# Two token blocks on half the partitions each, for the last six chunk pairs of an SSD scan fused with a PReLU MLP

## The chip, the cores and the metric

The kernel runs on one core of a Trainium2 chip. The metric is the device time of one execution in microseconds; before the change it is 359.88 us, the median of three runs (359.64 to 360.04). The engines are called TensorE (PE in the profile; PEld is its weight loading), VectorE (DVE), ScalarE (ACT), GpSimd (POOL) and SyncE (SP, which issues nearly all DMAs).

## The reference

Two blocks follow each other. The first is a state-space scan over 4 batches, 8 heads, 768 tokens, with a head width D of 32 and a state width N of 16. The reference walks it in chunks of 32 tokens; any chunk length gives the same numbers:

```
la  = log(clip(a, 1e-6, 1));  cum = cumsum(la)           # within the chunk
L   = exp(cum[i] - cum[j]) where i >= j, else 0          # decays, lower triangle
M   = (C B^T) * L                                        # gram times decays
y   = M x + (C state) * exp(cum)                         # within, and carried in
state = exp(sum la) * state + sum_j B_j x_j exp(cum_end - cum_j)
```

The second takes y as a matrix of 3072 tokens by 256 features: `h = y @ w_in` (256 by 2048), `g = max(h, 0) + alpha * min(h, 0)`, `out = g @ w_out` (2048 by 256). All data is float32, and the kernel's matmuls are float32 too: TensorE runs each as two passes, each with a weight load and a matmul instruction of its own.

## The kernel before, in words

**Chunks and pairs.** The scan's chunk here has Q = 128 tokens. There are 24 chunks, and the kernel works on them two at a time: 12 pairs (`gp`, NP = 12), three to a batch, pair 0 to 2 of batch 0 and so on. For each chunk and head it needs a 128 by 128 triangle: the decays L (function `half_decays`, which calls `scan_half`, L470) come from a scan on VectorE along the row `a` spread over all partitions (tile `abc`), to which an identity is added so that the product starts at 1 on the diagonal; the gram C B^T (`products_bc`, L599) comes from TensorE, the eight heads lying on the partitions, 16 state rows each, two heads to a 32-row tile of the array; VectorE multiplies the two into `dec` (L609). One instruction of each step covers full squares, the half above the diagonal included, which is zero.

**Outputs and states.** `y` (L628 and L636) is the sum of the carried-in part (masked state times decayed C, 64-row by 32-column tiles) and `x` times `dec` (128-row by 32-column tiles), for two chunks and eight heads, in two PSUM banks; ScalarE copies it into `xT` (L645). `added` (L513) forms the state that a chunk adds, from `x` and the weighted B (`bn`, made by GpSimd in `pair_loads`, L418); `states` (L526, L523) updates the running state, and GpSimd masks it by heads (`sm`, L529). `c_decayed` (L563) and `spread_c` (L560) make two forms of C. `turn_bc` (L477) transposes B and C of the next pair on VectorE and begins its scans. The result of `added` for the next pair lies in the free half of the second of the two `y` banks (`beside`).

**The MLP** is the main load of TensorE. For the first 512 tokens it is plain (`hidden`, L853, and `output`, L891); for the other five groups of 512 tokens (`g` = 1 to 5) it uses seven block products in place of eight in both matrix products (`quad`, L977 for the first and `product`, L952, for the second). A group has four quads (`z` = 0 to 3) of about 13.6 us each; GpSimd makes the sums that the seven products need (`token_sums`, L932; L1024 and L1034 for g).

**Order.** It is written out by hand: each engine runs its instructions in the order in which the program emits them. `pair` is a generator; the table `steps` and the calls at `j == 5` in `after(j)` say between which products of a quad the stages of a pair are put. In a group the even pair's stages fall in quads 0 and 1 and the odd pair's in 1 to 3. The order on TensorE at a pair's end is: carried-in part, products with x, and right behind them the added state of the next pair.

**Loads.** `load_pair` puts a pair's DMAs on SP at the start of quads 0 and 2: the decays of C (`ap`), B and x of each chunk with tokens on partitions, B and C again as rows of tokens for the transpose (L184), and by `load_spread` the row `a` broadcast to all partitions (`abc`, L137). SP is in order too: from quad 1 of group 2 on, the output stores of `finish` (L1114) stand ahead of a load and wait for their data. `bns[ahead]` makes the weighted B in the same quad as the load, at j = 9; `turn_bc` follows in the next quad.

**Row preparation** for batches 2 and 3 (`rows_clamp(1)`, `rows_scan(1)`, `rows_out(1)`, later `rows_turn(1)`) writes the clamped rows to DRAM for the spread loads, and turns the products of decays to the end of each chunk onto partitions (`prt`), on TensorE with one copy by ScalarE.

The functions that the change touches follow as they are before it.

Of the kernel before, what the change touches and what calls it, by code (L numbers as in the profile page):

```python
# [22 lines left out]
def kernel(  # L23
# [51 lines left out]
    HT = GT // 2  # L75
    NB = 2
    WQ = 256
    assert H * N == P and HD == d_model and KC == 2 and R == CPB == 6
    assert NCH % GC == 0 and GT == 512 and NF % 8 == 0 and d_model <= WQ

# [47 lines left out]
    def load_a(t, b, c, eng=nc.sync):  # L128
        first = a[b, 0:1, c * Q : (c + 2) * Q]
        eng.dma_start(out=t, in_=bass.AP(tensor=first.tensor, offset=first.offset,  # L130
                                             ap=[[S, H], [0, N], [1, 2 * Q]]))

    def load_spread(gp, b, c):

        for k, t in enumerate(loads["p", gp][1]):
            rows = scratch["z", b // 2].rearrange("(b h c) t -> b c h t", b=2, h=H)[b % 2, c + k]
            nc.sync.dma_start(out=t.rearrange("p (h t) -> p h t", h=H),  # L137
                              in_=rows.unsqueeze(0).to_broadcast([P, H, Q]))

    def load_pair(gp, decays=True):  # L140


        b, c = divmod(2 * gp, CPB)
        turned = gp > GC
        nat = ldx.tile([P, 3, 2, H * N], F32, name="nat")
        xt = ldx.tile([P, 2, HD], F32, name="xt")

        ap = ldx.tile([P, 2 * Q], F32, name="ap")
        if gp == 0:
            load_a(ap, b, c)  # L150
        elif gp >= NB:
            rows = scratch["pf", b // 2].rearrange("(b h c) t -> b h (c t)", b=2, h=H)
            rows = rows[b % 2, :, c * Q : (c + 2) * Q]
            nc.sync.dma_start(out=ap, in_=rows.unsqueeze(1).to_broadcast([H, N, 2 * Q]))
        if gp == 0:
            load_rows(0, nc.scalar)
            nc.sync.dma_start(out=al_n, in_=moe_alpha.rearrange("(k p) -> k p", p=P))
        abc = []
        later = []
        for k in range(2):  # L160
            ts = slice((c + k) * Q, (c + k + 1) * Q)
            for i, src in enumerate((B,) if turned else (B, C)):
                nc.sync.dma_start(out=nat[:, i, k].rearrange("p (h n) -> p h n", h=H),  # L163
                                  in_=src[b, :, ts, :].rearrange("h p n -> p h n"))

            def load_x(k=k, ts=ts):
                nc.sync.dma_start(out=xt[:, k].rearrange("p (h d) -> p h d", h=H),
                                  in_=x[b, :, ts, :].rearrange("h p d -> p h d"))

            if gp < NB:  # L170
                later.append(load_x)
            else:
                load_x()
        for load_x in later:
            load_x()
        if gp == 0:
            loads["a", 1] = prep.tile([P, 2 * Q], F32, name="a1")
            load_a(loads["a", 1], b, c + 2)
        for i, src in enumerate((B, C) if turned else ()):


            for e in range(2):
                first = src[b, e : e + 1, c * Q : (c + 2) * Q, :]
                nc.sync.dma_start(out=nat[:, 1 + e, i],  # L184
                                  in_=bass.AP(tensor=first.tensor, offset=first.offset,
                                              ap=[[2 * S * N, P // 32], [8 * N, 32], [1, 8 * N]]))
        for k in range(2 if gp >= NB else 0):
            abc.append(lda.tile([P, H * Q], F32, name="abc"))
        loads["p", gp] = nat, abc, xt, ap
        if decays:  # L190
            load_spread(gp, b, c)
# [170 lines left out]
    def identity_bank():  # L362
# [3 lines left out]
        nc.scalar.copy(out=m5_bank[0][:, HT:], in_=ident_h[:, :HT])  # L366
        ident_p.append(m5_bank[0][:, HT:])

    def rows_clamp(i):
        rows = loads.pop(("r", i))  # L370
        d0 = prep.tile([RW, Q + 1], F32, name="r0")
        nc.vector.tensor_scalar(out=d0[:, :Q], in0=rows, scalar1=1e-6, scalar2=1.0,
                                op0=ALU.max, op1=ALU.min)
        held[i] = d0

    def rows_scan(i):

        d0 = held[i]
        nc.vector.memset(d0[:, Q:], 0.0)
        pr = prep.tile([RW, Q], F32, name="pr")  # L380
        nc.vector.tensor_tensor_scan(out=pr[:, ::-1], data0=d0[:, 1:][:, ::-1],
                                     data1=ends[:RW, ::-1], initial=0.0,
                                     op0=ALU.mult, op1=ALU.add)
        return pr
# [1 line left out]
    def rows_out(i):  # L386


        d0 = held.pop(i)[:, :Q]
        rpf = prep.tile([RW, Q], F32, name="rpf")  # L390
        nc.vector.tensor_tensor_scan(out=rpf, data0=d0, data1=zeros[:RW], initial=1.0,
                                     op0=ALU.mult, op1=ALU.add)
        nc.vector.memset(d0[:, :1], 0.0)
        for key, t in (("z", d0), ("pf", rpf)):
            scratch[key, i] = dr.tile([RW, Q], F32, name=f"{key}{i}")
            nc.sync.dma_start(out=scratch[key, i], in_=t)

    def rows_turn(i, pr):
# [2 lines left out]
        nc.tensor.transpose(ps[:, :RW], pr, ident[:RW, :RW])  # L401
        if i == 0:
            nc.tensor.transpose(ps[:, RW : RW + NF], al_n, ident[:NF, :NF])
        t = bat.tile([P, RW], F32, name="prt")
        nc.scalar.copy(out=t, in_=ps[:, :RW])
        if i == 0:
            nc.scalar.copy(out=alpha, in_=ps[:, RW : RW + NF])
        prt[i] = t
# [1 line left out]
    def pair_loads(gp):  # L410
# [3 lines left out]

        bn = work.tile([P, 2, H * N], F32, name="bn")
        i, bi = divmod(b, 2)
        pj = prt[i].rearrange("p (b h c) -> p b c h", b=2, h=H)[:, bi, c : c + 2]
        nc.gpsimd.tensor_tensor(  # L418
            out=bn.rearrange("p k (h n) -> p k h n", h=H),
            in0=nat[:, 0].rearrange("p k (h n) -> p k h n", h=H),  # L420
# [41 lines left out]

    bcs = {}
    decs = {}

    def scan_half(dec, abc, k, w):
        dv = dec.rearrange("p k h t -> p k (h t)")
        for i in range(2):
            hs = slice((2 * w + i) * 2 * Q, (2 * w + i + 1) * 2 * Q)
            nc.vector.tensor_tensor_scan(out=dv[:, k, hs], data0=abc[k][:, hs],  # L470
# [13 lines left out]
    def pair(gp):  # L484
# [2 lines left out]
        nat, abc, xt, ap = loads["p", gp]  # L487
        last = c + 2 == CPB
        fine = gp >= 2 * GC // 2
        dec = decs.pop(gp) if gp in decs else work.tile([P, 2, H, Q], F32, name="dec")  # L490
        dv = dec.rearrange("p k h t -> p k (h t)")
        begun_scans = gp in bcs

        def decays(k):
# [10 lines left out]
        new = work.tile([P, 2, 2 * D], F32, name="state")  # L505
        sm = work.tile([P, 2, P], F32, name="sm")

        def added(dps):
            dps = dps[:, : 4 * D].rearrange("p (k m) -> p k m", k=2)
            for k in range(nk):  # L510
                for r in range(4):
# [2 lines left out]
                                     xt[:, k, 2 * r * D : 2 * (r + 1) * D],  # L514
                                     start=True, stop=True, tile_position=(0, 32 * r),
                                     skip_group_check=True)
            return dps

        def states(dps):
            for k in range(nk):  # L520
                old = state.get(b)
                if old is None:
                    nc.scalar.copy(out=new[:, k], in_=dps[:, k])  # L523
                else:
                    e = (k + 1) * Q - 1
                    nc.vector.scalar_tensor_tensor(out=new[:, k], in0=old, scalar=pf[:, e : e + 1],  # L526
                                                   in1=dps[:, k], op0=ALU.mult, op1=ALU.add)
                state[b] = new[:, k]
            nc.gpsimd.tensor_tensor(  # L529
                out=sm[:, :nk].rearrange("p k (g m) -> p k g m", g=2),  # L530
                in0=new[:, :nk].unsqueeze(2).to_broadcast([P, nk, 2, 2 * D]),
                in1=hmask.rearrange("p (g m) -> p g m", g=2).unsqueeze(1)
                .to_broadcast([P, nk, 2, 2 * D]), op=ALU.mult)
            st.extend(sm[:, k] for k in range(nk))
            masked[b] = st[-1]

        if fine:
            bn = bns.pop(gp) if gp in bns else pair_loads(gp)
            dps = added(beside.pop(gp) if gp in beside else ss_tile()[:, : 2 * Q])
            yield  # L540
            states(dps)
            yield
# [17 lines left out]
                nc.scalar.mul(cz[:, e].rearrange("p k t -> p (k t)"), ct, par[:, e : e + 1])  # L560

        def c_decayed():
            nc.gpsimd.tensor_tensor(out=cd.rearrange("p k t -> p (k t)"), in0=ct, in1=pf,  # L563
                                    op=ALU.mult)

        if not fine:
            bn = bns.pop(gp) if gp in bns else pair_loads(gp)
# [23 lines left out]

        def products_bc():
            small = 2 if fine else 3
            gram = {r: (ss_tile() if r < small else spare())
                    .rearrange("p (k h t) -> p k h t", k=2, h=2) for r in range(4)}
            for k in range(2):
                for r in range(4):
                    rs = slice(32 * r, 32 * r + 32)
# [6 lines left out]
            yield  # L605
        gram = products_bc()
        for i, r in enumerate((2, 3, 0, 1) if fine else (3, 2, 1, 0)):
            hs = slice(2 * r, 2 * r + 2)
            nc.vector.tensor_tensor(out=dec[:, :, hs], in0=gram[r], in1=dec[:, :, hs], op=ALU.mult)  # L609
            if i == 1:  # L610
                yield
        if fine and gp + 1 < NP:
            turn_bc(gp + 1)
        yield

# [1 line left out]
        ys = [ss_tile() for w in range(KC)]  # L617
        y = [t[:, : 2 * Q].rearrange("p (k t) -> p k t", k=2) for t in ys]
        if fine:
            beside[gp + 1] = ys[1][:, 2 * Q :]  # L620
        begun = False
        for k in range(2):
            if st[k] is not None:
                for q in range(4):
# [4 lines left out]
                                         stop=False, tile_position=(64 * w, 32 * q),  # L629
                                         skip_group_check=True)  # L630
                begun = True
        for k in range(2):
            for w in range(KC):
                for q in range(4):
                    h = 4 * w + q
# [6 lines left out]
        if q == 0:  # L642
            xts[g] = xtp.tile([P, KC, GT], F32, name="xT")
        for w in range(KC):
            nc.scalar.copy(out=xts[g][:, w, q * Q : (q + 2) * Q],  # L645
                           in_=y[w].rearrange("p k t -> p (k t)"))


    def first_two():
# [573 lines left out]
    for i in range(NZ * (NG - 1)):  # L1223
# [3 lines left out]
        def after(j, g=g, z=z, i=i, nxt=nxt):  # L1227
# [5 lines left out]
                    output(NF - LATE + f, half)  # L1233
            if (i, j) in ((0, 13), (1, 2)):
                store_first(i)
            for args in late_sums.get((i, j), ()):
                weight_sums(*args)
            if g > 1 and z == 0 and j in (7, 11, 13, 14):
# [57 lines left out]
```

## Time and profile before

| what | value |
|---|---|
| median of 3 runs | 359.88 us (359.64 to 360.04) |
| the profiled execution | 360.17 us |
| its span, first to last instruction | 358.0 us |
| granted TensorE clock | 1.000 |
| TensorE busy | 351.5 us, 98% of the span |
| VectorE busy | 248.1 us, 69% |
| ScalarE busy | 169.6 us, 47% |
| GpSimd busy | 203.5 us, 57% |
| DMA, mean rate | 88 GB/s |
| the stretch of pairs 6 to 11 (146.2 to 291.2 us) | DVE busy 101.48, POOL 73.33, ACT 64.29 us of 145.00 |

Each line of the profile below names an engine, a source line, an operation with output<-input by the program's tile names, the shape of the array tile for TensorE (rows*columns), and partitions x elements. In a timeline line the first number is the start in us from the start of the span, the second the time to the end of the group, and x is the number of instructions in it. A matmul's end is modelled; the distance from one start to the next says how fast TensorE goes. Waits between engines go over semaphores; an instruction that has to wait for more than one is preceded by a wait instruction of its own, which the engine's sequencer carries out while the array still works on what was handed over before.

### The profile page before, as it was taken

What the parts mean: (1) busy time and instruction counts of PE and PEld (TensorE: products, weight loads), DVE (VectorE), ACT (ScalarE), POOL (GpSimd) and SP (SyncE); (2) the same over time, 40 slices, a digit from 0 to 9 for tenths busy, and PEclk for the clock granted to TensorE, in tenths of its full rate; (3) what the DMA queues carried; (4) which work ended last, traced back from release to release, by engine and by line L of the source; (5) the groups of instructions that cost most, each with busy time, mean ns of one, the idle gap of its engine ahead of it and who ended that gap; (6) DMA issues with size and microseconds to landing.
All of it is one profiled execution on the core that took longest, in us unless ns stands there. A gap on an engine that the chain in (4) does not pass through costs nothing.

```text
span 358.0 us, 6719 instructions
## 1 busy us (share of the span) xinstructions
PE 351.5 (98%) x2509; PEld 286.5 (80%) x2509; DVE 248.1 (69%) x465; ACT 169.6 (47%) x367; POOL 203.5 (57%) x212
## 2 busy tenths in 40 slices
PE   8899999999999999999999999999999999999996
PEld 7676665678788788888888888888888888888884
DVE  7987986998747857858748858667867633643363
ACT  3677576536256255355245454345445345443431
POOL 4976668589839755725655725646626535434521
PEclk9999999999999999999999999999999999999999
DMA  6999998408266202005505504603601001001004
GB/s 107 203 191 322 286 243 222 130 16 180 85 145 127 80 2 61 0 2 86 150 1 79 156 4 68 169 1 63 173 4 29 2 2 29 0 2 30 0 0 88
DMA packets 111015, 31.66 MB, mean 88 GB/s; under 512 B 79288, under 2 KB 106888, under 8 KB 110984
## 3 DMA queue, kind: packets, MB, share of 16 engines
q1 hardware_dynamic: 110056, 31.00, 37.1%
q8 instruction: 19, 0.31, 0.4%
q10 hardware_dynamic: 928, 0.25, 0.3%
q14 instruction: 12, 0.10, 0.1%
HBM read 27.89 MB, written 3.34 MB: 87 GB/s over the span
## 4 chain that ended last, share of the span: by engine, by line
PE 95%; POOL 1%; DMA 1%; SPq 1%; DVE 0%; issue 0%; ACT 0%; POOLq 0%
PE bank L952 34%; PE hp L977 28%; PE bank L891 8%; PE hp L853 6%; PE ss L977 6%; PE ss L636 3%; PE ss L599 2%; PE hp L868 2%; PE ss L628 1%; DMA nat<-in_C_dram 1%; PE bank L453 1%; PE ss L513 1%; PE hp L599 0%; SPq L163 0%; POOL w_in L291 0%
## 5 line engine op out<-in xcount | busy, mean ns | idle before, releaser
L1034 POOL TENSOR_TENSOR gt<-gt 128x512 f32<-128x512 f32 x58 | 74.2, 1280 | 21.2 <-DVE gt L962 16.4
L952 PE MATMUL bank<-gt,w_out 128*128 128x256 f32 x320 | 83.5, 381 | 0.0
L952 PEld LDWEIGHTS bank<-gt,w_out 128*128 128x128 f32 x320 | 60.1, 190 | 10.3 <-issue 2.3
L1024 POOL TENSOR_TENSOR gt<-gt 128x512 f32<-128x512 f32 x20 | 25.4, 1272 | 67.3 <-DVE gt L962 61.9
L962 DVE SCALAR_TENSOR_TENSOR gt<-hp,s_mul,gt 128x256 f32<-128x256 f32 x96 | 42.0, 479 | 29.9 <-ACT gt L960 27.3
L952 PE MATMUL bank<-gt,ws 128*128 128x256 f32 x240 | 59.5, 379 | 0.0
L960 ACT ACTIVATE gt<-hp,s_alpha 128x256 f32<-128x256 f32 x96 | 40.4, 472 | 39.3 <-PE hp L977 25.9
L952 PEld LDWEIGHTS bank<-gt,ws 128*128 128x128 f32 x240 | 45.6, 190 | 6.2
L470 DVE TENSOR_TENSOR_SCAN dec<-abc,bank 128x256 f32<-128x256 f32 x80 | 48.4, 659 | 0.0
L977 PE MATMUL hp<-xs,w_in 128*128 128x256 f32 x160 | 41.9, 384 | 0.0
L977 PE MATMUL hp<-xs,ws 128*128 128x256 f32 x160 | 41.2, 380 | 0.0
L1003 DVE TENSOR_TENSOR hp<-hp,u 128x512 f32<-128x512 f32 x20 | 13.9, 696 | 28.7 <-ACT u L1001 28.7
L977 PEld LDWEIGHTS hp<-xs,ws 128*128 128x128 f32 x160 | 30.3, 190 | 4.3 <-POOL xs L932 0.2
L977 PEld LDWEIGHTS hp<-xs,w_in 128*128 128x128 f32 x160 | 29.7, 190 | 4.6 <-issue 0.2
L891 PE MATMUL bank<-w_out,gt 128*128 128x256 f32 x128 | 31.1, 385 | 0.0
L891 PEld LDWEIGHTS bank<-w_out,gt 128*128 128x128 f32 x128 | 23.6, 190 | 6.8 <-issue 2.9
L977 PE MATMUL ss<-xT,w_in 128*128 128x256 f32 x96 | 24.6, 379 | 0.0
L853 PE MATMUL hp<-xT,w_in 128*128 128x512 f32 x48 | 22.7, 596 | 0.1
L529 POOL TENSOR_TENSOR sm<-state,bmask 128x256 f32<-128x256 f32 (+1 forms) x10 | 6.2, 620 | 29.0 <-DVE state L526 29.0
L992 ACT COPY m<-hp 128x512 f32<-128x512 f32 x8 | 4.7, 586 | 37.8 <-PE hp L977 37.8
L1001 ACT COPY u<-hp 128x512 f32<-128x512 f32 x20 | 11.7, 586 | 19.9 <-PE hp L977 19.9
L977 PE MATMUL hp<-xT,ws 128*128 128x256 f32 x80 | 20.5, 379 | 0.0
(179 smaller groups left out, 583.3 us busy)
## 6 DMA issues: line engine op xcount, KB each, us to landing
abc<-z SPq DMA_DIRECT2D x20, 512.0 KB
raw<-in_moe_w_in_dram SPq DMA_DIRECT2D x8, 512.0 KB
raw<-in_moe_w_out_dram SPq DMA_DIRECT2D x8, 512.0 KB
xt<-in_x_dram SPq DMA_DIRECT2D x24, 128.0 KB
nat<-in_B_dram SPq DMA_DIRECT2D x38, 64.0 KB
out_dram<-o_sb SPq DMA_DIRECT2D x32, 64.0 KB
nat<-in_C_dram SPq DMA_DIRECT2D x24, 64.0 KB
ap<-pf SPq DMA_DIRECT2D x11, 128.0 KB
```

The source lines that it names most:

```text
L470: nc.vector.tensor_tensor_scan(out=dv[:, k, hs], data0=abc[k][:, hs], data1=ident_p[0], initial=0.0, op0=ALU.mult, op1=ALU.add)
L636: nc.tensor.matmul(y[w][32 * q : 32 * q + 32, k], xt[:, k, h * D : (h + 1) * D], dec[:, k, h], start=False, stop=True, tile_position=(0, 3 ...
L853: nc.tensor.matmul(hp, w_in[:, k, f * P : (f + 1) * P], xts[g][:, k], start=(k == 0), stop=(k == KC - 1))
L891: nc.tensor.matmul(pos[0][t // 2][:, t % 2], gt[:, t * Q : (t + 1) * Q], w_out[:, f], start=(f == 0 and t % 2 == 0), stop=(f == NF - 1), s ...
L952: nc.tensor.matmul(ms[g][i][:, h], w, blocks[g, z][n][:, p], start=(q == 0 and h == 0), stop=(q == NQ - 1), skip_group_check=True)
L960: nc.scalar.mul(o[:, p], h[:, p], s_alpha[:, fs[p]])
L962: nc.vector.scalar_tensor_tensor(out=o[:, p], in0=h[:, p], scalar=s_mul[:, fs[p]], in1=o[:, p], op0=ALU.mult, op1=ALU.max)
L977: nc.tensor.matmul(to[:, p], w(2 * z + p), b, start=start and p == 0, stop=True, skip_group_check=True)
L1001: nc.scalar.copy(out=u2, in_=A)
L1003: nc.vector.tensor_tensor(out=Y, in0=Y, in1=u2, op=ALU.add)
L1024: nc.gpsimd.tensor_tensor(out=tc_, in0=g22, in1=g12, op=ALU.subtract)
L1034: eng.tensor_tensor(out=o, in0=x0, in1=x1, op=ALU.subtract)
```

## The change

For pairs 6 to 11 (`HALF = NP // 2`) a head's chunk no longer lies on 128 partitions. Its 128 tokens j are split into two blocks of 64; both blocks of a head lie on the same 64 partitions, one behind the other along the free axis: the first with all 128 columns i, the second with the last 64 columns alone (SQ = 192 columns in all). The other 64 partitions hold the same for a head of the other chunk of the pair or the other group of four heads: partition half `v` has chunk `v ^ w` of head group `w`.

So the scans have 192 columns in place of 256 for two heads, a gram bank 384 in place of 512, and `x` times `dec` takes two matmuls of 64 rows, one with 128 and one with 64 columns, where it took one of 128 rows and 128 columns. The matmuls are issued on tiles of 32*64 (gram) and 64*32 (products with x, and the added state, whose sum over tokens now takes two matmuls). What has to do with chunks lies swapped in the second chunk, so masked state, decayed C and state updates are done in more and smaller instructions, the loads of B, x and `abc` in smaller DMAs (16 for B and x where there were four, four for `abc` where there were two), and the copy of `y` in four instructions where there were two. The identity in PSUM, the rows for `abc` and `prt` get the new order once.

```diff
+    HQ = Q // 2
+    SQ = Q + HQ
+    HALF = NP // 2
...
+    def load_tokens(dst, src, t0):
+        d = dst.rearrange("p j (h w) -> p j h w", h=H)
+        for v in range(2):
+            for w in range(2):
+                for j in range(2):
+                    t = t0 + (v ^ w) * Q + j * HQ
+                    nc.sync.dma_start(out=d[HQ * v : HQ * (v + 1), j, 4 * w : 4 * w + 4],
+                                      in_=src[4 * w : 4 * w + 4, t : t + HQ, :]
+                                      .rearrange("h p w -> p h w"))
     def load_spread(gp, b, c):
-        for k, t in enumerate(loads["p", gp][1]):
+        for w, t in enumerate(loads["p", gp][1] if gp >= HALF else ()):
+            rows = scratch["z", b // 2].rearrange("(b h c) t -> b c h t", b=2, h=H)
+            for v in range(2):
+                nc.sync.dma_start(
+                    out=t[HQ * v : HQ * (v + 1), : 4 * SQ].rearrange("p (h t) -> p h t", h=4),
+                    in_=rows[b % 2, c + (v ^ w), 4 * w : 4 * w + 4].unsqueeze(0)
+                    .to_broadcast([HQ, 4, SQ]))
...
+        if gp >= HALF:
+            load_tokens(nat[:, 0], B[b], c * Q)
+            load_tokens(xt, x[b], c * Q)
-        for k in range(2):
+        for k in range(2 if gp < HALF else 0):
...
+    def halve_identity():
+        for s in range(2):
+            nc.scalar.copy(
+                out=ident_p[0][HQ:].rearrange("p (a s t) -> p s a t", a=2, s=2)[:, s],
+                in_=ident[HQ:, HQ * (1 - s) : HQ * (2 - s)].unsqueeze(1).to_broadcast([HQ, 2, HQ]))
+    def rows_swapped():
+        prs = prep.tile([RW, Q], F32, name="rpf")
+        for h in range(2):
+            nc.scalar.copy(out=prs[:, HQ * h : HQ * (h + 1)],
+                           in_=held["pr"][:, HQ * (1 - h) : HQ * (2 - h)])
+        held["prs"] = prs
...
     def rows_turn(i, pr):
...
+        else:
+            nc.tensor.transpose(ps[:, RW : 2 * RW], held["prs"], ident[:RW, :RW])
...
+        for v in range(2 if i else 0):
+            vs = slice(HQ * v, HQ * (v + 1))
+            for j in range(2):
+                for w in range(2):
+                    nc.scalar.copy(
+                        out=t[vs].rearrange("p (j b m h) -> p j b h m", j=2, b=2, h=H)
+                        [:, j, :, 4 * w : 4 * w + 4],
+                        in_=ps[vs, (j ^ v) * RW : ((j ^ v) + 1) * RW]
...
     def scan_half(dec, abc, k, w):
+        if ident_p and halved:
+            dv = dec.rearrange("p k h t -> p (k h t)")
+            for i in range(2):
+                s = (2 * w + i) * SQ
+                o = (4 * k + 2 * w + i) * SQ
+                nc.vector.tensor_tensor_scan(out=dv[:, o : o + SQ], data0=abc[k][:, s : s + SQ],
+                                             data1=ident_p[0][:, :SQ], initial=0.0,
+                                             op0=ALU.mult, op1=ALU.add)
+            return
...
+        def added_halves(banks):
+            dps = [t[:, : 4 * D].rearrange("p (k m) -> p k m", k=2) for t in banks]
+            for j in range(2):
+                for r in range(4):
+                    rs, hs = slice(32 * r, 32 * r + 32), slice(2 * r * D, 2 * (r + 1) * D)
+                    for v in range(2):
+                        vs, k = slice(HQ * v, HQ * (v + 1)), v ^ r // 2
+                        if k < nk:
+                            nc.tensor.matmul(dps[v][rs, k], bn[vs, j, rs], xt[vs, j, hs],
+                                             start=False, stop=j == 1,
+                                             tile_position=(HQ * v, 32 * r),
+                                             skip_group_check=True)
...
         def states(dps):
...
+                for ps, rs in dps[k]:
...
+            for ks in (slice(k, k + 1) for k in range(nk)) if half else (slice(0, nk),):
+                n = ks.stop - ks.start
+                for frm, to in halves(1 - ks.start if half else 0):
+                    nc.gpsimd.tensor_tensor(
+                        out=sm[to, ks].rearrange("p k (g m) -> p k g m", g=2),
...
         def c_decayed():
+            for ks in (slice(0, Q), slice(Q, 2 * Q)) if half else (slice(0, 2 * Q),):
+                for frm, to in halves(ks.start):
+                    nc.gpsimd.tensor_tensor(out=cd.rearrange("p k t -> p (k t)")[to, ks],
+                                            in0=ct[frm, ks], in1=pf[frm, ks], op=ALU.mult)
...
         def products_bc():
+            for e in range(2 if half else 0):
+                for j in range(2):
+                    for r in range(4):
+                        rs = slice(32 * r, 32 * r + 32)
+                        for v in range(2):
+                            k = v ^ r // 2
+                            o = e * SQ + j * Q
+                            nc.tensor.matmul(gram[r][HQ * v : HQ * (v + 1), o : o + Q - HQ * j],
+                                             bh[rs, k, HQ * j : HQ * (j + 1)],
+                                             cz[rs, e, k, HQ * j :], start=True, stop=True,
+                                             tile_position=(32 * r, HQ * v),
+                                             skip_group_check=True)
...
+            if gp + 1 == HALF:
+                halve_identity()
+                halved.append(True)
             turn_bc(gp + 1)
...
-        for k in range(2):
+        for k in range(2 if half else 0):
+            for j in range(2):
+                for q in range(4):
+                    qs = slice(32 * q, 32 * q + 32)
+                    for w in range(KC):
+                        ws = slice(64 * w, 64 * w + 64)
+                        h = 4 * (w ^ k) + q
+                        nc.tensor.matmul(y[w][qs, k, HQ * j :], xt[ws, j, h * D : (h + 1) * D],
+                                         by_head[ws, h, Q * j : Q + HQ * j], start=False,
+                                         stop=j == 1, tile_position=(64 * w, 32 * q),
+                                         skip_group_check=True)
...
         for w in range(KC):
+            for k in range(2 if half else 0):
+                nc.scalar.copy(out=xts[g][:, w ^ k, (q + k) * Q : (q + k + 1) * Q], in_=y[w][:, k])
...
+            if (i, j) == (1, 3):
+                rows_swapped()
```

## The prediction

> **What bounds the kernel now.** I read the page's busy times and its chain first, then the tensor engine's timeline around one pair, then single instruction records. Busy times and chain:
>
> ```profile
> PE 351.5 (98%) x2509; PEld 286.5 (80%) x2509; DVE 248.1 (69%) x465; ACT 169.6 (47%) x367; POOL 203.5 (57%) x212
> ...
> PE 95%; POOL 1%; DMA 1%; SPq 1%; DVE 0%; issue 0%; ACT 0%; POOLq 0%
> ```
>
> TensorE (PE) sets the end; the others count where they make it wait or change its instructions. Its timeline, pair 8's gram and then its outputs with pair 9's added state:
>
> ```profile
> 200.92 0.48 PE L599 MATMUL ss<-cz,bc 32*128 32x256 f32 x2
> ...
> 201.69 0.38 PE L599 MATMUL hp<-cz,bc 32*128 32x256 f32 x2
> 202.00 0.70 PE L952 MATMUL bank<-gt,w_out 128*128 128x256 f32 x2
> ...
> 207.38 0.67 PE L628 MATMUL ss<-cd,sm 64*32 64x128 f32 x32
> 207.98 1.08 PE L636 MATMUL ss<-dec,xt 128*32 128x128 f32 x32
> 208.87 0.41 PE L513 MATMUL ss<-xt,bn 128*32 128x64 f32 x16
> ```
>
> See the tile shapes (32*128 is rows by columns of the array) and the counts, two instructions for each matmul of the program. Single records show rounds: 4 or 8 matmuls on different tiles start 7 ns apart, and the next round follows after 216 ns (256 columns), 109.5 ns (128) or 56 ns (64). From L628 to L636 the shape changes and 0.14 us pass beyond a round; from L636 to L513 nothing.
>
> Records of waits show how fast PE's sequencer hands over instructions. Three times two waits with 8 instructions between them are 125 ns apart (28.10, 28.22 and 58.51 us); once, with 16 between, 182 ns (17.09 us). So an instruction takes (182-125)/8 = 7.1 ns, a wait 68 ns. The wait for L513 is at 208.24, its first weight load 34 instructions later: the sequencer runs 34 ahead, and no more. A round of eight tiles is 16 instructions with the loads, 114 ns at that pace.
>
> **The change, part by part.** Six pairs (6 to 11, from 146 to 291 us).
>
> Gram, L599. Before: 16 matmuls, first issue to the end of the last round 0.97 us. After: 64 on 32*64 tiles, by columns 2 x 2 x (0.1095+0.056) = 0.66, and 0.05 for the first load. By hand-over: 128 instructions, 34 of them waiting, 94 x 7.1 = 0.67, plus a last round 0.06 and the first matmuls' 0.05. I take 0.77: 0.2 saved, 1.2 in six.
>
> Outputs and added state. By columns L636 falls from 8 x 0.1095 = 0.88 to 0.66, and the shape change before it (0.14, and 0.02 of first loading) goes, since both are then 64*32. But the instructions double. Pair 8: before 0.60+0.90+0.22 = 1.72; after 64+128+64 = 256, so 222 x 7.1 = 1.58, a wait 0.07, a last round 0.06: 1.71. By columns it would be 1.35. Pairs 6 and 9 (one chunk carried in): 0.38+0.90+0.22 = 1.50 against 190 x 7.1+0.13 = 1.48. Pairs 7 and 10 (one chunk added for the next): 0.60+0.90+0.11 = 1.61 against 1.48. Pair 11 (nothing added): 1.50 against 158 x 7.1+0.06 = 1.18. Saved: 0.01+0.04+0.26+0.32 = 0.63. Pair 5's outputs stay at 128*32 and pair 6's added state does not: a new shape change, 0.16 lost. A second transpose in `rows_turn`: 0.11 lost (L550's transposes are 0.109 apart). TensorE: 1.2+0.63-0.27 = 1.56 saved.
>
> Two statements of the Trainium skill bear on this, apart from the sum. "TensorEngine Tiling (Array Packing)", Instruction Overhead, gives each matmul about 60 cycles and advises against tiling a dimension that is already small; at 2.4 GHz 64 of them in series are an estimated 1.6 us, and the gram would lose 0.6 instead of gaining 0.2. The rows are against it here: starts on different tiles are 7 ns apart. "TensorE: Matmul & The Clock Gate", on the array's architecture, gives TensorE a queue of 64; with 64 ready instead of 34, pair 8's block would take 192 x 7.1+0.13 = 1.49 and gain 0.2; the records show 34.
>
> VectorE. The eight scans go from 256 columns (L470, 659 ns) to 192: with L712 (512 columns, 1207 ns) a column is 2.1 ns, so 522 ns, 1.1 us less a pair; the four multiplies (685 ns, L609) to about 555, 0.5 less; up to two further state updates of 279 ns (L526), 0.6 more. 1 us less a pair off the path: worth nothing.
>
> ScalarE and GpSimd. Four copies of outputs of about 266 ns (between 239 for 96 columns, L405, and 373 for 256, L645) for two: 0.3 more. Mask and decayed C become three instructions each of about 457 ns (L529's 128x128 row) for 730 ns: 0.64 more, twice. Behind the mask at 210.2 GpSimd was idle 3.0 us, behind the decayed C at 221.4 4.4 us: covered. Where token sums follow (238.4 to 241.5), they end about 1 us later, and their reader is at 245.2: covered by 2.7. If a cover were gone, each would cost up to that 0.6 or 1 us a pair. `rows_turn`: eight copies of some 0.18 (alpha's 128x16: 178 ns) for one of 0.24, from 117.0, and the gram at 118.68 needs that bank: 0 to 0.2 late, I take 0.1. The identity's and the swapped rows' copies, four of 0.2 to 0.4, run in ScalarE's idle 4 us; VectorE's first scan of pair 6 waits for the former, behind a transpose of 1.10 (L477) that covers them: nothing.
>
> SP and DMA, the part with the widest bounds. Pair 9's load:
>
> ```profile
> 192.60 0.61 SPq L154 DMA_DIRECT2D ap<-pf  x1
> 193.26 0.46 SPq L163 DMA_DIRECT2D nat<-in_B_dram  x1
> 193.82 0.53 SPq L167 DMA_DIRECT2D xt<-in_x_dram  x1
> 194.39 0.73 SPq L163 DMA_DIRECT2D nat<-in_B_dram  x1
> 195.16 0.58 SPq L167 DMA_DIRECT2D xt<-in_x_dram  x1
> 195.79 1.26 SPq L184 DMA_DIRECT2D nat<-in_B_dram  x2
> 197.09 1.12 SPq L184 DMA_DIRECT2D nat<-in_C_dram  x2
> 198.25 2.01 SPq L137 DMA_DIRECT2D abc<-z  x2
> ```
>
> The four DMAs for B and x (2.5 us) become 16, the last two four; queued behind the 16 are B and C turned, and the decays. Landings by the records: last C at 204.14, first decays 205.57. VectorE transposes at 205.18 (1.10), scans twice, then adds at 207.26 (L1003, 0.70), and TensorE reads that sum at 210.18. So the last C may land as late as 210.18-0.1-1.10-1.04-0.70 = 207.2, about 207.0 with TensorE 0.2 earlier. The four turned DMAs land 0.95 us apart, the first packet 1.2 us after issue; with d for one of the 16, C lands at 193.26+16d+1.2+3.8, up to 1.7 more where decays mix in, as they did. The floor of d is 0.34 (the shorter stores, L1114)+0.05 between issues: 204.5 to 206.2, no wait. The ceiling is L184's 0.58: 207.5 to 209.2, 0.5 to 2.2 us for each of four pairs. The nearest row has as many descriptors, L222's raw weights, 0.37 to 0.47+0.05, so about 0.47: 205.8 to 207.5, wait 0 to 0.5. Pairs 6 and 7 load earlier (96.8 and 109.2), and are safe; 8 to 11 start behind the output stores. I take 0.1 each, 0.4, bounds 0 and 9. GpSimd's weighted B (200.29) needs only the first eight, landed by about 199.7 at 0.47: no wait. Stores behind the load are 27 us away.
>
> Sum: -1.56+0.1+0.4 = -1.06. The profiled execution took 360.17 us (span 358.0, 2.2 around it): 359.1. The median shown is 0.3 below that execution, so 358.8.
>
> **Rivals.** (1) Columns alone decide, hand-over does not: six grams save 0.26, the blocks 0.37, 0.37, 0.37, 0.26, 0.26 and 0.38; 1.56+2.01-0.27 = 3.3 less, 356.6. For it: within L628 and L513 rounds keep the pace of their columns. Against: L628 needs only 30 instructions beyond the 34 ready. (2) Slower: the late turned C. From d = 0.55 (C at 207.1 to 208.8) VectorE's in-order queue holds up L1003, and TensorE stands 0.1 to 1.8 us in each of four pairs. With 1.2 each: 4.8-1.46, about 363.2; it decides against the change at 0.4 a pair. Against it: VectorE starts that transpose some 0.3 us sooner and has no other late input. (3) A wash: hand-over in a long run is 8 ns instead of 7.1, since matmuls there carry waits of their own. The grams lose 94 x 0.9 = 0.08 each and five of the six blocks 0.17 to 0.2: 1.4 of the 1.56 go, with 0.5 elsewhere 360.2. That the work does not shrink at all is excluded: the shapes are in the program.
>
> **How the numbers follow.** A measurement here tells 0.2%, 0.7 us, from no change. My case: 0.45, its own range 358.1 to 359.7. Rival 1: 0.12. Rival 2: 0.22, from 360.0 to 366. Rival 3: 0.21, 359.3 to 361. Faster: 0.36 of mine, 0.12, 0.04 of rival 3: 0.52. Same: 0.09+0.04+0.08 = 0.21. Slower: 0.18+0.09 = 0.27. The range goes from 356.8, which leaves out half of rival 1 (0.06), to 362.4, which leaves out the dearer half of rival 2 (0.11).
>
> **What would show it.** Rounds of 16 instructions some 114 ns apart in L636's successor once the first 34 are through, not 56; gram 0.2 shorter; no 0.14 gap between the two output lines; B and x issued within 7.5 us; VectorE's transpose of pairs 8 to 11 not later than 2 us after now. Wrong if the hand-over paces differently from 7.1 ns, or if the small DMAs cost what L184's do.

## The result: slower by 8.4%, and the profile after

The changed kernel takes 389.98 us (median of 5 runs, 389.40 to 391.17) against 359.88 us: the ratio is 1.0843, 95% interval 1.082 to 1.0867. The forecast was 358.8, with a range that ended at 362.4. The profiled execution has a span of 387.7 us, 29.7 more than before.

The page of the changed kernel: busy time and share of each engine, the granted clock in 40 slices, the chain of work that ended last, and one of the costliest groups (busy us, mean ns, then idle time ahead of it and what ended that).

```profile
PE 359.8 (93%) x3070; PEld 294.6 (76%) x3070; DVE 242.6 (63%) x474; ACT 171.2 (44%) x392; POOL 210.7 (54%) x234
...
PEclk9999999999999999999699989989996999999999
...
PE 68%; SPq 15%; DMA 6%; POOL 3%; issue 3%; DVE 3%; ACT 1%; POOLq 0%; DVEq 0%; ACTq 0%
...
L1120 PE MATMUL hp<-xT,ws 128*128 128x256 f32 x80 | 24.7, 438 | 20.9 <-DVE hp L1146 20.9
```

TensorE's part of the chain falls from 95% to 68%. What came in is SP's issuing of DMAs (15%) and the DMAs (6%). TensorE now stands 20.9 us ahead of one group of matmuls, and in four places the clock row is under full speed. The waits of the changed kernel (engine, tile and line, what it waited for: us in total, how often, the longest) say who waits for whom:

```profile
DVE bc L549 <- DMA nat<-in_C_dram: 31.2, 4, 7.9
PEld hp L1120 <- DVE hp L1146: 22.5, 4, 5.9
PE hp L1120 <- DVE hp L1146: 20.9, 4, 5.5
POOL bn L480 <- DMA nat<-in_B_dram: 3.4, 2, 2.8
DVE dec L536 <- DMA abc<-z: 1.6, 4, 0.6
```

VectorE's two waits and TensorE's wait come four times each, in the turns of pairs 8, 9, 10 and 11. VectorE waits for the turned C, then for the decays; in its in-order queue the sum L1146 (L1003 before) stands behind both, and TensorE waits for that sum. Here is the first of the four, in the timeline of the changed kernel (start, length to the end of the group, engine, line, instruction, count; idle time ahead in brackets):

```profile
184.35 1.10 DVE L549 STREAM_TRANSPOSE bc<-nat 128x512 f32<-128x512 f32 x1 [7.77 <-DMA nat<-in_C_dram]
186.04 1.00 DVE L536 TENSOR_TENSOR_SCAN dec<-abc,bank 128x192 f32<-128x192 f32 x2 [0.59 <-DMA abc<-z]
186.96 0.67 DVE L1146 TENSOR_TENSOR hp<-hp,u 128x512 f32<-128x512 f32 x1
187.69 2.07 PE L1120 MATMUL hp<-xT,ws 128*128 128x256 f32 x4 [4.98 <-DVE hp L1146]
189.55 2.99 PE L1095 MATMUL bank<-gt,ws 128*128 128x256 f32 x8
```

Why C is late is in SyncE's own timeline of the same turn:

```profile
163.11 1.98 SPq L1257 DMA_DIRECT2D out_dram<-o_sb  x4
165.19 0.64 SPq L179 DMA_DIRECT2D ap<-pf  x1
165.87 5.23 SPq L147 DMA_DIRECT2D nat<-in_B_dram  x8
171.20 6.01 SPq L147 DMA_DIRECT2D xt<-in_x_dram  x8
177.26 1.18 SPq L212 DMA_DIRECT2D nat<-in_B_dram  x2
178.48 1.12 SPq L212 DMA_DIRECT2D nat<-in_C_dram  x2
```

B and x take SyncE 11.3 us (165.87 to 177.2) where the four larger DMAs of before took 2.5. In the single records one small DMA holds SyncE 0.615 us, the next starts 0.045 us later: 0.66 us each, the same for B's 16 KB and, where nothing holds them up, x's 32 KB (in this turn one of x's eight was held for 1.42). The turned C is issued behind them.

The standing has a second price. The changed kernel in two windows right after one another (length, busy time of each engine with its instructions, granted clock, DMA share, GB/s):

```profile
184.94:187.69 2.75, 0.00 (x1) 0.01 (x1) 2.15 (x5) 0.00 (x0) 0.00 (x0) 0.50 0.19 44
187.69:191.77 4.08, 4.08 (x10) 3.27 (x11) 2.09 (x6) 1.66 (x5) 3.59 (x6) 0.50 0.00 0
```

The clock falls to 0.5 while TensorE stands and stays there for the first 4.08 us in which it works again: ten matmuls in 4.08 us, where at the 216 ns of the full clock nineteen would fit. The clock records have four such stretches, of 6.83, 3.41, 3.41 and 6.83 us. In all that is 20.5 us at half clock, in some 17 of which TensorE worked, so they cost an estimated 8.5 us.

So the 29.7 us fall into two parts. TensorE's busy time rises by 8.3 us (351.5 to 359.8), and its time outside that by 21.4 (6.5 to 27.9), of which the four stands are 20.9.

### The profile page after: what moved, and what is told of

Read it like the earlier page. It is cut to its first block, busy times and chain, and to the rows that moved or that the text cites. A ratio compares the mean times of both kernels' runs of the same rounds, so it can differ in the third digit from the quotient of the medians.

```text
span 387.7 us, 8020 instructions
## 1 busy us (share of the span) xinstructions
PE 359.8 (93%) x3070; PEld 294.6 (76%) x3070; DVE 242.6 (63%) x474; ACT 171.2 (44%) x392; POOL 210.7 (54%) x234
## 4 chain that ended last, share of the span: by engine, by line
PE 68%; SPq 15%; DMA 6%; POOL 3%; issue 3%; DVE 3%; ACT 1%; POOLq 0%; DVEq 0%; ACTq 0%
PE bank L1095 23%; PE hp L1120 20%; SPq L147 9%; PE bank L1034 7%; PE hp L996 5%; DMA abc<-z 5%; PE ss L1120 4%; SPq L212 2%; POOL gt L1177 2%; SPq L156 2%; PE hp L1011 2%; DMA nat<-in_C_dram 1%; PE ss L776 1%; DVE gt L1105 1%; PE ss L757 1%
## 5 line engine op out<-in xcount | busy, mean ns | idle before, releaser
L1177 POOL TENSOR_TENSOR gt<-gt 128x512 f32<-128x512 f32 x58 | 74.1, 1278 | 25.3 <-DVE gt L1105 20.5
L1095 PE MATMUL bank<-gt,ws 128*128 128x256 f32 x240 | 63.7, 400 | 0.0
L1095 PEld LDWEIGHTS bank<-gt,ws 128*128 128x128 f32 x240 | 49.1, 204 | 7.8
L1120 PE MATMUL hp<-xT,ws 128*128 128x256 f32 x80 | 24.7, 438 | 20.9 <-DVE hp L1146 20.9
L631 POOL TENSOR_TENSOR sm<-state,bmask 64x128 f32<-64x128 f32 (+2 forms) x20 | 9.6, 480 | 50.0 <-DVE state L624 40.8
L1120 PEld LDWEIGHTS hp<-xT,ws 128*128 128x128 f32 x80 | 16.9, 217 | 24.8 <-DVE hp L1146 22.5
L1146 DVE TENSOR_TENSOR hp<-hp,u 128x512 f32<-128x512 f32 x20 | 13.9, 694 | 32.1 <-ACT u L1144 32.1
L549 DVE STREAM_TRANSPOSE bc<-nat 128x512 f32<-128x512 f32 x7 | 7.7, 1102 | 31.2 <-DMA nat<-in_C_dram 31.2
L536 DVE TENSOR_TENSOR_SCAN dec<-abc,bank 128x192 f32<-128x192 f32 x48 | 22.9, 527 | 1.6 <-DMA abc<-z 1.6
```

The costliest lines, as they stand in the source:

```text
L536: nc.vector.tensor_tensor_scan(out=dv[:, o : o + SQ], data0=abc[k][:, s : s + SQ], data1=ident_p[0][:, :SQ], initial=0.0, op0=ALU.mult, op ...
L631: nc.gpsimd.tensor_tensor(out=sm[to, ks].rearrange("p k (g m) -> p k g m", g=2), in0=new[frm, ks].unsqueeze(2) .to_broadcast([frm.stop - f ...
L1095: nc.tensor.matmul(ms[g][i][:, h], w, blocks[g, z][n][:, p], start=(q == 0 and h == 0), stop=(q == NQ - 1), skip_group_check=True)
L1120: nc.tensor.matmul(to[:, p], w(2 * z + p), b, start=start and p == 0, stop=True, skip_group_check=True)
L1146: nc.vector.tensor_tensor(out=Y, in0=Y, in1=u2, op=ALU.add)
L1177: eng.tensor_tensor(out=o, in0=x0, in1=x1, op=ALU.subtract)
```

## The experiments

**Load earlier.** If late loads are the whole cause, the changed kernel is cured by issuing each pair's loads one quad sooner, with nothing else touched:

```
-        if z == 0 and nxt < NP:
-            load_pair(nxt + 1)
-        if z == 2 and nxt + 2 < NP:
+        if i == 0:
+            load_pair(nxt + 1)
+        if z == 1 and nxt + 2 < NP:
             load_pair(nxt + 2)
+        if z == 3 and nxt + 3 < NP:
+            load_pair(nxt + 3)
```

> The changed kernel, with each load of a pair from pair 6 on issued one quad (13.7 us) earlier, ahead of the output stores that it stood behind. Theory (late loads: 16 small DMAs at 0.66 us each on SP push the turned B and C of pairs 8 to 11 8 us back, VectorE stands at its transpose, TensorE at VectorE's sum): the four waits of 5.4 us on TensorE and the half clock behind them go, 359.3 us (358.8 to 360.0); the transposes of pairs 8 to 11 wait for nothing. Rival (the layout itself costs it, by twice the instructions on TensorE and the smaller ones elsewhere): 385 to 390 us, as before. Rival (the DMA engines can't move the many small pieces): the waits stay or shrink in part, 365 to 385 us.

Measured: 359.74 us (359.38 to 360.39, 12 runs), ratio to the kernel before 0.9985, interval 0.9969 to 1.0001. Its page:

```profile
PE 350.9 (98%) x3070; PEld 289.6 (81%) x3070; DVE 243.0 (68%) x474; ACT 171.4 (48%) x392; POOL 211.1 (59%) x234
...
PE 94%; POOL 1%; DMA 1%; SPq 1%; DVE 1%; issue 1%; ACT 1%; POOLq 0%
```

All four stands are gone and the clock is 1.0. The same 3070 matmuls are busy 8.9 us less than in the changed kernel: that is the half clock, in size what was estimated above. With the loads in time the new layout is worth nothing that can be told from zero. (The kernel before, run again beside these, took 360.08 us, and 360.12 beside the two runs with x moved; the ratios are to these.)

**The small DMAs alone.** The opposite test puts the small DMAs into the kernel before, for pairs 6 to 11, and leaves the old layout and all its arithmetic. Eight DMAs for each of B and x, 64 partitions by four heads:

```
+        if gp >= NP // 2:
+            for dst, src in ((nat[:, 0], B), (xt, x)):
+                for k in range(2):
+                    d = dst[:, k].rearrange("p (h w) -> p h w", h=H)
+                    for v in range(2):
+                        for w in range(2):
+                            t = (c + k) * Q + 64 * v
+                            nc.sync.dma_start(out=d[64 * v : 64 * v + 64, 4 * w : 4 * w + 4],
+                                              in_=src[b, 4 * w : 4 * w + 4, t : t + 64, :]
+                                              .rearrange("h p w -> p h w"))
-        for k in range(2):
+        for k in range(2 if gp < NP // 2 else 0):
```

> The kernel before, with nothing of its computation changed, but with B and x of pairs 6 to 11 loaded in 8 DMAs each, 64 partitions by 4 heads, to the same places. Theory (late loads): 16 DMAs take 10.6 us on SP where four took 2.5, so the loads of pairs 8 to 11 are 8 us late as in the changed kernel, and the time goes to 387 to 392 us with four waits of some 5 us on TensorE. Rival (the layout): 359.2 to 360.6 us, as before.

Measured: 386.74 us (384.16 to 388.74, 4 runs), ratio 1.0734, interval 1.0695 to 1.0773. SyncE's timeline and the waits of this kernel:

```profile
165.48 5.24 SPq L167 DMA_DIRECT2D nat<-in_B_dram  x8
170.82 5.23 SPq L167 DMA_DIRECT2D xt<-in_x_dram  x8
176.09 1.16 SPq L194 DMA_DIRECT2D nat<-in_B_dram  x2
```

```profile
DVE bc L487 <- DMA nat<-in_C_dram: 24.1, 4, 6.3
PEld hp L987 <- DVE hp L1013: 18.5, 4, 5.2
```

Again 0.66 us a DMA, the same four waits, and TensorE stands in the same four places, for 3.50 to 4.78 us where it was 4.98 to 5.50; the time is 0.3 us under what was expected. The span is 27.2 us longer than before, of which TensorE's busy time, with the kernel before's 2509 matmuls, is 9.9 (361.4 against 351.5) and its idle time 17.3. The split of the loads costs 27 of the 30 us with no part of the new arithmetic in it. The rest is not traced singly; that the four decay DMAs, two of them here, come behind the C and that VectorE waited 31.2 instead of 24.1 us for C fits it.

**Earlier loads in the kernel before.** To be sure that the cure in the first run is not a gain of its own, the kernel before got the same edit.

> The kernel before, with its loads one quad earlier as in e1_early and nothing else. Theory: its loads landed in time (last turned C at 204.1 for a transpose at 205.2), so nothing is won: 359.5 to 360.2 us. If early loads alone gain something, what e1_early shows isn't the layout's gain: below 359.2 us.

Measured: 359.94 us (359.55 to 360.95, 12 runs), ratio 0.9999, interval 0.9988 to 1.001. Nothing was waiting there.

**x last.** The changed kernel with the same DMAs in another order: B, the turned B and C, the decays, then x. If C's place in SyncE's line is what counts, the wait must move to x; if C's transfers are slow by themselves, it must stay.

```
         if gp >= HALF:
             load_tokens(nat[:, 0], B[b], c * Q)
-            load_tokens(xt, x[b], c * Q)
...
         if decays:
             load_spread(gp, b, c)
+        if gp >= HALF:
+            load_tokens(xt, x[b], c * Q)
```

> The changed kernel with x's eight DMAs issued last of a pair's loads instead of in front of C's. Theory (SyncE's issue line is the bottleneck: each small DMA holds it 0.66 us, so a pair's last-issued input is ready some 20 us after the first issue): C comes 5.3 us earlier, VectorE's waits for C at the turn, now 7.9 us each, shrink to under 2.6 us and TensorE no longer stands at the sum of L1146; but x is issued some 19 us after the loads begin (163.1 to 182.3 us in the changed kernel's times) and TensorE asks for it at about 181 us, so it stands at the added states instead, 2 to 3.5 us a pair, in four or five pairs. Idle stretches below 3.4 us leave the granted clock at 1.0 or lose little of it: about 370 us, 366 to 378. Rival (it is C's transfers themselves, their 2 KB rows, that come late under load, not their place in the line): the wait for C stays about 8 us a pair, time 385 to 395 us.

Measured: 378.78 us (376.96 to 380.90, 4 runs), ratio 1.0521, interval 1.0477 to 1.0565. Its waits:

```profile
PEld ss L599 <- DMA xt<-in_x_dram: 11.6, 9, 3.0
PE ss L599 <- DMA xt<-in_x_dram: 11.3, 11, 2.9
DVE bc L550 <- DMA nat<-in_C_dram: 6.0, 4, 2.5
```

The wait moved as foretold: VectorE's waits for C shrink from 31.2 to 6.0 us, and TensorE stands at the added states (L599), 11.3 us in four turns, for an x that is issued last. The time is 0.8 us above the top of what was expected, and the clock is the reason. Stands of 2 to 3.5 us were expected to cost little of it, but the records have the clock at 0.5 for 3.41, 6.83 and 3.41 us in or behind three of the four turns, and TensorE is busy 359.5 us, not 350.9 as with early loads. Only the last stand, 2.85 us long, left it at 1.0. So the length of one stand does not tell whether the clock falls.

What tells it is where a stand lies. In every run here the clock changes only at whole steps of 3.413 us, counted from its first record, whatever TensorE does in between. Here are three such steps of this run (length, then busy time of TensorE, its weight loads, VectorE, ScalarE and GpSimd, clock, DMA share, GB/s); the first is the one that the stretch of 6.83 us follows, the other two share the last stand:

```profile
213.28:216.69 3.41, 1.67 (x97) 1.21 (x74) 1.33 (x3) 0.00 (x0) 0.00 (x0) 1.00 0.32 50
278.14:281.55 3.41, 2.03 (x103) 1.53 (x101) 1.61 (x4) 0.34 (x1) 0.00 (x0) 1.00 0.40 69
281.55:284.96 3.41, 1.94 (x19) 1.69 (x20) 0.94 (x3) 0.77 (x4) 0.59 (x2) 1.00 0.08 11
```

The last stand is cut in two by the end of a step, 1.38 and 1.47 us of standing on either side, and the clock stays. In the eleven steps after which it fell in the turns of pairs 8 to 11 (four in the changed kernel, four with split loads, three here) TensorE stood 1.75 to 3.41 us; in the steps of all runs after which it stayed at 1.0, at most 1.77. So in these runs standing for about half a step halves the clock at the step's end. The ends of matmuls are modelled, and the border is no sharper than that.

**x issued by ScalarE.** Last, is the 0.66 us the issuing engine's own time, or that of something which all queues share? x's eight DMAs go to ScalarE, in a stretch in which, in the turn shown below, it has nothing to do:

```
-            load_tokens(xt, x[b], c * Q)
+            held["x"] = xt, x[b], c * Q
...
         def after(j, g=g, z=z, i=i, nxt=nxt):
+            if j == 10 and "x" in held:
+                load_tokens(*held.pop("x"), nc.scalar)
```

> The changed kernel with x's eight DMAs of a pair issued by ScalarE, in a stretch of 5.1 us in which it has nothing to do (171.4 to 176.6 us in the changed kernel's times), and all else as it is. Theory (the 0.66 us is the time of the engine that issues, one DMA after the other on SyncE; two engines issue side by side): SyncE's line is 5.3 us shorter, C is turned 5 to 6 us earlier, the waits of VectorE for C fall from 7.9 to about 2 us, those of TensorE from 5.5 us to 0 to 0.7 us, clock 1.0 nearly throughout: 360 to 364 us, if ScalarE's copies after that stretch are not held up by more than 1 us. Rival (what takes 0.66 us is shared by all queues, such as the DMA engines or the making of descriptors): SyncE's remaining DMAs become slower while ScalarE issues, C is hardly earlier, and the time stays at 380 to 392 us.

Measured: 363.48 us (362.74 to 363.99, 4 runs), ratio 1.0098, interval 1.0078 to 1.0118. ScalarE's and SyncE's timelines of that kernel in one turn:

```profile
173.59 0.61 ACTq L147 DMA_DIRECT2D xt<-in_x_dram  x1
174.23 5.71 ACTq L147 DMA_DIRECT2D xt<-in_x_dram  x7
```

```profile
168.87 5.25 SPq L147 DMA_DIRECT2D nat<-in_B_dram  x8
174.16 1.18 SPq L212 DMA_DIRECT2D nat<-in_B_dram  x2
175.38 1.26 SPq L212 DMA_DIRECT2D nat<-in_C_dram  x2
```

Here ScalarE and SyncE issue beside each other, and SyncE's turned DMAs take 1.18 and 1.26 us, hardly more than alone (1.18 and 1.12 in the changed kernel). C comes earlier, no stand for it is left, and the time falls by 26.5 us. What remains of loss is one place. In pair 6's load ScalarE's DMAs were in front of a copy for 7.5 us, and TensorE waited for that copy for some 2.6 us near 126 us; without it the kernel would be at about 360.9 (363.48 - 2.6, an estimate). "DMA: Bandwidth & Descriptors" of the Trainium skill, in Issuing engines are not separate DMA queues, says that a second issuing engine only saves the sequencer's time to initiate a DMA, which is usually small beside the DMA. This run agrees with the first half; but here the time to initiate was the whole matter: it took eight times 0.66 us off SyncE's line.

**A shorter gram.** With the loads in time, TensorE decides again. The changed gram loads the same weights twice, once for each chunk e; one matmul over both halves the count (64 to 32), on top of the earlier loads:

```
-            for e in range(2 if half else 0):
-                for j in range(2):
...
+            for j in range(2 if half else 0):
+                for r in range(4):
+                    rs = slice(32 * r, 32 * r + 32)
+                    for v in range(2):
+                        k = v ^ r // 2
+                        o = gram[r][HQ * v : HQ * (v + 1), : 2 * SQ].rearrange(
+                            "p (e t) -> p e t", e=2)[:, :, j * Q : Q + HQ * j]
+                        nc.tensor.matmul(o, bh[rs, k, HQ * j : HQ * (j + 1)],
+                                         cz[rs, :, k, HQ * j :], start=True, stop=True,
+                                         tile_position=(32 * r, HQ * v),
+                                         skip_group_check=True)
```

> e1_early, and the gram's two matmuls that share a weight tile (the two heads of a 32-row tile) are one, with 256 or 128 columns: 16 matmuls and their loads in place of 32, the same columns. Theory (TensorE's sequencer hands over an instruction in some 8 ns, so in the changed kernel the 128 instructions of a gram decide and not its columns): the gram goes from 1.03 us to about 0.82, 1.2 us less in six pairs, 358.1 us (357.6 to 358.6). Rival (columns decide already): no difference to e1_early, within 0.2 us.

Measured: 358.64 us (358.24 to 360.64, 12 runs), ratio 0.997, interval 0.9953 to 0.9988: faster than both kernels, if by little, and 0.04 us above the range that was expected. From the gram's first matmul to the next one of the MLP it is 0.836 us now, 1.033 in the changed kernel and 1.076 before. Six times 0.197 is 1.18 us, and the medians of this run and the first differ by 1.10, though their single runs overlap.

## Why the prediction was wrong, step by step

**The step that failed is the price d of a small DMA.** The prediction took 0.47 from L222's raw weights, "the nearest row has as many descriptors", and put the ceiling at L184's 0.58. It measured 0.66, above the ceiling. As many descriptors in a DMA did not make the nearest row: a chunk of B on 128 partitions, with four times the descriptors, took 0.46 before, a quarter of it on 64 partitions takes 0.615. The prediction's own view of pair 9's load held a row with the right price, the decays' DMA (L154): 0.61 us, and 0.66 to the next issue (192.60 to 193.26). The sixteen take 11.4 us in the turn shown (10.6 to 11.7 in the four) instead of the 7.5 that d = 0.47 makes of them, 3.9 us more.

**The landing of the turned C**, taken as 1.2 + 3.8 = 5.0 us from the issue of the first turned DMA and up to 1.7 more, was 7.0 (177.26 to about 184.3): 2.0 more than the value, 0.3 more than the bound. The term was short for the kernel before already: by the prediction's own figures C landed there 8.35 us after the first turned DMA was issued (195.79 to 204.14), while the large pieces of B and x, issued just ahead of it, were still landing.

**The wait** was to begin at 13.9 us from the issue of B (207.2 - 193.26). C came at 18.4, and the decays, to which no wait was given, add 0.6: about 5.1 by the prediction's own formula with the measured terms, 4.98 to 5.5 in the waits. So mechanism and formula held, and 0.1 us a pair became over 5. This is rival 2, whose place and point of decision (d = 0.55) were right, but whose price was worked out at a d just past that point. A chance of 0.22 for it was too small with a ceiling that lay so near the point and was no bound at all.

**The granted clock was in no term.** It costs another 8 to 10 us: 8.9 in busy time between the changed kernel and its run with early loads, 9.9 between the kernel before and the one with split loads. "TensorE: Matmul & The Clock Gate" of the Trainium skill, in The HAM clock gate, says that the clock is halved after at least one idle window of about 3.4 us, and that these windows run free. The steps of 3.413 us in these records agree with the windows. But such a step need not be idle throughout: of the eleven falls three followed a step in which TensorE only stood, eight a step with 1.75 to 2.53 us of standing.

**TensorE's own saving was to be 1.56 us, and is about a third of that.** The gram saves 0.04 each, not 0.2, by the distance from its first matmul to the next of the MLP. Towards the end of a gram, when what was handed over ahead is used up, the records have weight loads 16.5 ns apart, two instructions each: a hand-over of 8.3 ns, not the 7.1 that the waits had given. 94 x 8.3 + 0.11 = 0.89 us against a measured 0.93 (1.033, less the 0.106 us by which 1.076 stands above the prediction's 0.97 for the gram before). This is rival 3. The outputs with the added states saved 0.55 in six pairs (0.63 was said), though spread differently: 0.06 to 0.08 in five pairs and 0.19 in pair 11. Pair 5's new change of shape cost 0.16 as said (1.832 to 1.992), and the gap of 0.14 between the two lines of outputs is gone. 0.26 + 0.55 - 0.16 - 0.11 makes 0.54, where the last is `rows_turn` as it was said. In the run with early loads three of the output blocks (pairs 7 to 9) are 0.14 to 0.23 us longer than in the changed kernel, through short stalls inside them; what causes these was not tried, and with them nothing of the saving is left.

**What held.** VectorE's 5.5 us less work (248.1 to 242.6; 1 us a pair was said) is worth nothing. The smaller and more numerous instructions of ScalarE and GpSimd make TensorE wait for nothing new in the run with early loads. Pairs 6 and 7, whose loads are early, do not wait. GpSimd's weighted B, said not to wait, waited 0.6 us in one of the six pairs (at 242.5 us), and nobody waited for it; the 2.8 us in the table of waits lies at the kernel's start, ahead of anything that was changed.

Of what was to be seen, three signs pointed to the failed step: B and x issued in 11.3 us and not within 7.5, VectorE's transpose 6.6 us later after B's issue than before (18.5 against 11.9) and not at most 2, and the condition "if the small DMAs cost what L184's do".

## What to carry to other kernels

An edit that cuts one transfer into many is priced by the queue that issues them: count the DMAs, take the dearest row of the issuing engine, not the nearest-looking, and see who is queued behind them. Where the sum comes near the point at which an engine starts to stand, price the case beyond that point in full, with the clock that TensorE loses. Order, lead time and a second issuing engine are cheap remedies, and they show at once whether issuing was the cause.

## What the runs showed of the hardware

- A DMA on 64 partitions with 256 short pieces takes its issuing engine 0.615 us and 0.045 to the next, with pieces of 64 or 128 bytes alike; one on 128 partitions with 1024 pieces of 64 bytes took 0.46, where nothing held it. Why the smaller one is dearer stays open.
- ScalarE and SyncE issue side by side and hardly slow each other: in the turn shown ScalarE's eight DMAs took 0.60 to 0.84 us each, SyncE's four turned ones 0.56 to 0.64, where alone they took 0.54 to 0.57.
- The granted clock changes on a grid of 3.413 us. It was halved after eleven steps in which TensorE stood 1.75 to 3.41 us, and stayed after steps with up to 1.77. It was back after one step where TensorE stood no more than 0.30 us in it (four times), and after two where it stood 0.60 or more in the first (seven times).
- TensorE takes over about 8.3 ns for each instruction in a long run of small matmuls on different tiles, with some 34 handed over ahead (so many starts lie between one wait before the change, at 208.24 us, and the first weight load behind it). Half the matmuls at twice the columns shortened such a run by 19% (1.033 to 0.836 us).
